# Attention: VectorE's lower parts from odd slots issued behind the next slot's softmax steps

## The chip, the cores and the metric

The kernel runs on one core of one Trainium2 chip. The metric is the device time of one execution in microseconds. Below, TensorE is also PE (matmuls) and PEld (its weight loads), VectorE is DVE, ScalarE is ACT, GpSimd is POOL, and SP is the engine that issues most DMAs. Each engine works through its own instructions in the order in which the program lists them.

## What is computed

Attention over 4 batches, 8 heads, 576 positions and head dimension 64, with a learned bias for each pair of positions, feeds a gated two-layer block over 2304 tokens:

```python
scores = scale * np.matmul(q, k.transpose(0, 1, 3, 2))
h = np.maximum(x @ w1 + b1, 0.0)          # x: log distance over log position
scores = scores + (h @ w2).transpose(2, 0, 1)[None]
attn = np.exp(scores - np.max(scores, axis=-1, keepdims=True))
attn = attn / (np.sum(attn, axis=-1, keepdims=True) + 1e-09)
out = np.matmul(attn, v)
...
gate = 1.0 / (1.0 + np.exp(-(x @ w_gate)))
return gate * (x @ w_val) @ w_out
```

## The kernel before

The program has three stages: the bias tables (to about 115 us), the attention (115 to about 405 us) and the gated block (from about 390 us to the end). The change touches the attention alone.

The attention works through 16 **units**, each a pair of heads of one batch, and each unit through 9 **slots** (`n = 9 * u + s`). The slots 0, 2, 4 and 6 compute the scores of two blocks of 128 rows, one for each head (12 matmuls of line 627 into two `sc` tiles); slot 8 computes the last 64 rows of both heads in one tile (6 matmuls of line 616); the odd slots compute no scores. There are two `sc` buffers, so the scores of a slot can start only when the softmax steps of the slot with scores before it have read theirs.

A **softmax step** (`soft`, lines 631 to 650) is, for one tile, a DVE instruction that adds the bias and takes the row's extreme (line 643, with a short read of the accumulator), for the second head a small addition (line 647), and the exponential with its row sum on ACT (line 648).

Two slots later `turn` brings the block's exponentials into the layout that the second product needs. Blocks of even slots and the one of slot 8 are transposed on PE (line 672, into one of three `pt` buffers); ACT writes the **upper part** in 16 bits to `at` (line 561), and DVE later writes the **lower part**, the rest (line 562). Blocks of odd slots (the second head's) are cut into two parts by POOL (lines 555 and 666, `cr`) and transposed by DMAs that SP issues (line 667). So of the lower parts that DVE writes, these come from odd slots: in slot 1 the two halves of the unit before's block 8; in slot 3 what `tail` issues for that unit (a lower part of 64 x 128 and the row sums' reciprocals `rt`, line 696, which SP stores to `rs`); in slots 5 and 7 the lower parts of V (`vv`, line 603), whose upper parts ACT writes on line 602 at the end of the slot.

The second product (line 732) of the unit before is spread over the slots in four groups of nine matmuls, 3 or 6 in a slot; each group fills the one `acc` buffer, which ACT empties to `xe` (line 736). The whole is written under a manual schedule: the order of the loop's code is the order on each engine.

Of the kernel before, what the change touches and what calls it, by code (L numbers as in the profile page):

```python
# [28 lines left out]
LAG, WSTEP, VSTEP, TAIL = 2, 2, (5, 7), 3  # L29
# [143 lines left out]
def tile_kernel(ctx, tc, q, k, v, small, w_gate, w_val, w_out, steps, lpos, xtab, lx, out, phases="0AB"):  # L173
# [7 lines left out]
    with ExitStack() as right, ExitStack() as att:  # L181
# [16 lines left out]

        sizes = {}
        attn = attention(tc, att, q, k, v, biases, biasL, ident, xs, rs, sizes, extra)  # L200
        next(attn)
        with tc.manual_schedule():
# [314 lines left out]
def attention(tc, att, q, k, v, biases, biasL, ident, xs, rs, sizes, extra):  # L517
# [15 lines left out]
    def load_k(u):  # L533

        p, b = units[u]
        qkraw[u, "kr"] = t = raw.tile([128, S], F32, name="kr")
        nc.sync.dma_start(out=t, in_=k[b, 2 * p:2 * p + 2].rearrange("h d s -> (h d) s"))

    def load_q(u):

        p, b = units[u]
        qkraw[u, "qr"] = t = raw.tile([128, S + 64], F32, name="qr")
        nc.sync.dma_start(out=t, in_=q[b, p].rearrange("h d s -> (h d) s"))

    def load_v(u):
        p, b = units[u]
        vraw[u] = raw.tile([128, 2, 5, D], F32, name="vr")
        nc.sync.dma_start(out=vraw[u], in_=v[b, p])
# [19 lines left out]
    def prep_k(u):  # L568
        kt[u] = t = two.tile([128, 2, S], F32R, name="k")
        pool_split(t[:, 0], t[:, 1], qkraw[u, "kr"])  # L570

    def prep_q(u):
        qt[u] = o = two.tile([128, 2, S + 64], F32R, name="part")
        pool_split(o[:, 0], o[:, 1], qkraw[u, "qr"])
# [23 lines left out]
    def split_v(u, h):  # L598
        if h == 0:
            vsplit[u] = vp.tile([128, 2, 5, 2, D], F16, name="vv")  # L600
        t, vv = vraw[u][:, h], vsplit[u][:, h]
        nc.scalar.activation(out=vv[:, :, 0], in_=t, func=AF.Copy, scale=sizes["up"])
        return lambda: nc.vector.scalar_tensor_tensor(out=vv[:, :, 1], in0=t, scalar=sizes["up"], in1=vv[:, :, 0], op0=ALU.mult, op1=ALU.subtract)
# [3 lines left out]
    def score(n):  # L607
        u, s = divmod(n, 9)
        ks, qs = kt[u], qt[u]
        if s == 0:  # L610
            state[u] = [st.tile([128, 9], F32, name="sm"), None, {}]
        if s == 8:
            ps = ps_s.tile([128, 2, 512], F32, name="sc")
            for i, (l, r) in enumerate(TERMS):
                for e in range(2):
                    nc.tensor.matmul(out=ps[:, e, 0:HF], lhsT=qs[:, l, 512:640], rhs=ks[:, r, HF * e:HF * e + HF],
                                     start=(i == 0), stop=(i == len(TERMS) - 1))
            return [soft(u, s, ps)]
        if s % 2:
            return []  # L620
        it = TURN[s][1]
        pair = [ps_s.tile([128, 2, 512], F32, name="sc") for _ in range(2)]
        for i, (l, r) in enumerate(TERMS):
            for e in range(2):
                for h in range(2):
                    rows = slice(64 * h, 64 * h + 64)
                    nc.tensor.matmul(out=pair[h][:, e, 0:HF], lhsT=qs[rows, l, 128 * it:128 * it + 128], rhs=ks[rows, r, HF * e:HF * e + HF],  # L627
                                     start=(i == 0), stop=(i == len(TERMS) - 1))
        return [soft(u, s + h, pair[h]) for h in range(2)]
# [22 lines left out]
    def turn(n):  # L652

        u, s = divmod(n, 9)
        p, b = units[u]
        if s == 0:
            state[u][1] = atp.tile([128, 2, 9, S], F16, name="at")
        sm, at, ens = state[u]
        h, it = TURN[s] if s < 8 else (0, 4)
        en = ens[4 * h + it if s < 8 else 8]  # L660
        i = slice(128 * it, 128 * it + 128)
        if s in CROSS:
            t = crp.tile([128, 2 * S], F16, name="cr")
            copy(t[:, 0:S], en)
            for a, z in ((640, slice(0, 512)), (S, slice(512, S))):
                nc.gpsimd.tensor_tensor(out=t[:, a:a + z.stop - z.start], in0=en[:, z], in1=t[:, z], op=ALU.subtract)  # L666
            crossed.append((n + LAG + XLAG, lambda: nc.sync.dma_start_transpose(out=at[:, h, :, i], in_=t)))
            return []
        after = []
        pt = ps_t.tile([128, 4, 128], F32, name="pt")  # L670
        for J in range(4):
            nc.tensor.transpose(pt[:, J], en[:, 128 * J:128 * J + 128], ident)  # L672
        if s == 8:
            return [split(at[:, h, 0:4, 512:576], at[:, h, 5:9, 512:576], pt[:, :, 64 * h:64 * h + 64]) for h in range(2)]
        after.append(split(at[:, h, 0:4, i], at[:, h, 5:9, i], pt))
        if it == 3:
            pt = ps_t.tile([128, 4, 128], F32, name="pt")
            for e in range(4):
                nc.tensor.transpose(pt[0:64, e], ens[4 * h + e][:, 512:576], ident)
            after.append(split(at[0:64, h, 4, 0:512], at[64:128, h, 4, 0:512], pt[0:64].rearrange("p e i -> p (e i)")))  # L680
        return after

    def tail(u):
        sm, at, ens = state[u]
        pt = ps_t.tile([128, 4, 128], F32, name="pt")
        nc.tensor.transpose(pt[0:64, 0], ens[8][:, 512:576], ident)
        last = normal(u, pt)
        return [split(at[0:64, :, 4, 512:576], at[64:128, :, 4, 512:576], pt[0:64, 0].rearrange("p (h i) -> p h i", h=2)), last]
# [14 lines left out]
    def invert(u):  # L703
        sm = state[u][0]

        def both():
            nc.vector.tensor_tensor(out=sm, in0=sm, in1=sizes["tiny"], op=ALU.add)
            nc.vector.reciprocal(out=sm, in_=sm)

        return both  # L710
# [35 lines left out]
    crossed = []  # L746
    with tc.manual_schedule():
        work = iter(())
        after, due, loads = [], [], []
        for n in range(9 * NU + LAG + 1):  # L750
            u, s = divmod(n, 9)
            softs = score(n) if n < 9 * NU else []
            inverse = invert(u - 1) if s == 0 and u > 0 else None
            later = turn(n - LAG) if LAG <= n < 9 * NU + LAG else []
            if s == TAIL and u > 0 or n == 9 * NU + LAG:
                later += tail(u - 1)
            if s == KSTEP and u + 1 < NU:
                prep_k(u + 1)
                if u + 2 < NU:
                    loads.append(lambda z=u + 2: load_k(z))  # L760
            if s == QSTEP and u + 1 < NU:
                prep_q(u + 1)
                if u + 2 < NU:
                    loads.append(lambda z=u + 2: load_q(z))
            for f in after:
                f()
            for f in due:
                f()
            for f in softs:
                f()  # L770
            due, loads = loads, []
            while crossed and (crossed[0][0] <= n or n == 9 * NU + LAG):
                crossed.pop(0)[1]()
            after = later
            if inverse:
                inverse()
            if s == WSTEP and 0 < u < NU:
                work = products(u - 1)
            if n == 9 * NU + LAG - 1:
                work = products(u - 1)  # L780
            for _ in range(FILL[s] if n < 9 * NU else 9 if n < 9 * NU + LAG else 0):
                f = next(work, None)
                if f:
                    f()
            if s in VSTEP and u < NU:
                after.append(split_v(u, VSTEP.index(s)))
                if s == VSTEP[1] and u + 1 < NU:
                    loads.append(lambda z=u + 1: load_v(z))
            extra(n)
        for f in after:  # L790
            f()
        for f in work:
            if f:
                f()
# [562 lines left out]
```

## Time and profile before

| | |
|---|---|
| time, median of 3 runs | 825.13 us (824.43 to 825.15) |
| the profiled execution's own time | 824.43 us, with a span of 822.6 us |
| PE, DVE, ACT, POOL busy over the span | 92%, 78%, 69%, 44% |
| attention's first and last softmax step on DVE | 114.7 us, 389.1 us |

The span is the part of the profiled execution in which engines work; what lies around it is 1.8 us. The busy shares are means over three stages with different limits, so the stage that is changed has to be read on its own. In the rows below that give busy time by stretch, the columns are the stretch, its length, the busy us (and instructions) of PE, PEld, DVE, ACT and POOL, then TensorE's granted clock, the DMA engines' busy share and GB/s.

### The profile page before, as it was taken

Reading aid. Unit: us, or ns where it says so; the run is one execution under the profiler, and the core shown is the slowest. Engines: PE = TensorE matmul, PEld = TensorE weight load, DVE = VectorE, ACT = ScalarE, POOL = GpSimd, SP = SyncE. Lnnn points to the kernel's source line nnn. Section 1 sums busy time; section 2 is a strip of 40 time slices with the busy share of each in tenths; the row PEclk is TensorE's granted clock in tenths of the full one; section 3 lists DMA queues with packets and bytes.
Section 4 is the critical chain, followed back from the end, with each engine's and each line's share of the span. In section 5 each row is a group of like instructions: output and inputs, shape, how many; then the busy total and the mean of one; then the engine's idle time right before and its main releaser. Section 6 shows DMA issues by size and latency. Waiting matters only on the chain. (4 is left out here: it accounts for less than half of the span.)

```text
span 822.6 us, 17293 instructions
## 1 busy us (share of the span) xinstructions
PE 756.1 (92%) x6343; PEld 548.1 (67%) x6343; DVE 642.6 (78%) x1362; ACT 564.6 (69%) x1206; POOL 362.8 (44%) x451
## 2 busy tenths in 40 slices
PE   7999878888888898788899999998999999999997
PEld 4888866666666666566799999984555555555553
DVE  6788877777778777888469889888998887777762
ACT  5887737877777777678657656476667666766553
POOL 2345448678777787784101111044743331533200
PEclk8999988999999999999999999999999999999999
DMA  5478315877687577886989884247621121522102
GB/s 193 152 192 186 108 44 140 161 161 169 145 180 165 142 178 168 212 210 157 245 295 285 248 227 133 90 138 210 180 93 64 60 77 47 184 78 78 52 1 77
DMA packets 137236, 121.84 MB, mean 148 GB/s; under 512 B 82368, under 2 KB 106048, under 8 KB 137152
## 3 DMA queue, kind: packets, MB, share of 16 engines
q1 hardware_dynamic: 130560, 112.03, 49.2%
q0 software_dynamic: 4672, 5.77, 4.8%
q10 hardware_dynamic: 1920, 2.95, 1.1%
q8 instruction: 49, 0.80, 0.4%
q14 instruction: 35, 0.29, 0.1%
HBM read 80.80 MB, written 23.67 MB: 127 GB/s over the span
## 5 line engine op out<-in xcount | busy, mean ns | idle before, releaser
L1158 PEld LDWEIGHTS <-wv 128*128 128x128 f16 x1008 | 98.1, 98 | 84.4 <-issue 9.4
L648 ACT ACTIVATE en<-en,mn 128x576 f32<-128x576 f32 x144 | 111.8, 777 | 57.6 <-DVE mn L643 55.8
L627 PE MATMUL sc<-k,part 64*128 64x288 f32 x768 | 95.8, 329 | 21.8 <-DVE mn L643 18.0
L1158 PE MATMUL pg<-xq,wv 128*128 128x384 f16 x576 | 109.3, 326 | 2.9 <-ACT c L1184 2.1
L1116 POOL TENSOR_TENSOR ws<-wm 128x256 f32<-128x256 f32 x44 | 43.5, 989 | 152.0 <-DMA wm<-scratch 151.3
L627 PEld LDWEIGHTS sc<-k,part 64*128 64x128 f32 x768 | 67.4, 195 | 50.6 <-DVE mn L643 43.5
L666 POOL TENSOR_TENSOR cr<-en,cr 128x512 f16<-128x512 f32 (+1 forms) x128 | 96.7, 776 | 5.3
L643 DVE CUSTOM_DVE_ANT_0 en<-sc,bias 128x576 f32<-128x576 f32 x128 | 91.3, 749 | 4.1 <-PE sc L627 3.7
L562 DVE SCALAR_TENSOR_TENSOR at<-pt,at 128x512 f16<-128x512 f32 (+3 forms) x128 | 71.3, 568 | 23.8 <-ACT at L561 19.9
L732 PE MATMUL acc<-at,vv 128*128 128x288 f16 x540 | 81.3, 287 | 7.2 <-ACT xe L736 6.2
L1005 PE MATMUL po<-wo,gh 128*128 128x512 f16 x288 | 85.7, 379 | 0.0
L1158 PE MATMUL pu<-xq,wv 128*128 128x384 f16 x432 | 82.0, 326 | 1.9 <-DVE c L1164 1.9
L1057 POOL DMA_DIRECT2D xt<-xs x32 | 27.2, 1093 | 110.7 <-DMA xt<-xs 110.5
L555 POOL TENSOR_SCALAR cr<-en 128x576 f16<-128x576 f32 x64 | 44.5, 695 | 67.9 <-DMA at<-cr 35.4
L732 PEld LDWEIGHTS <-vv 128*128 128x128 f16 x576 | 56.3, 98 | 26.3 <-issue 13.6
L1164 DVE TENSOR_TENSOR c<-pu,c 128x384 f32<-128x384 f32 x72 | 39.9, 554 | 42.3 <-PE pu L1158 29.1
L427 PE MATMUL bps<-cfs,ind 128*128 128x64 bf16 x1458 | 67.5, 193 | 3.2 <-DVE bias L443 1.7
L408 ACT ACTIVATE ind<-y 128x576 bf16<-128x576 f32 x100 | 62.4, 651 | 11.1 <-PE y L403 8.3
L427 PEld LDWEIGHTS <-ind 128*128 128x128 bf16 x1458 | 58.8, 98 | 9.7 <-issue 3.0
L561 ACT ACTIVATE at<-pt 128x512 f16<-128x512 f32 (+3 forms) x128 | 59.9, 493 | 5.1 <-PE pt L672 2.3
L1176 ACT ACTIVATE gh<-c 128x384 f16<-128x384 f32 x48 | 25.1, 523 | 53.9 <-DVE c L1174 52.5
L672 PE MATMUL pt<-ident,en 128*128 128x128 f32 x320 | 54.1, 293 | 1.4 <-ACT en L648 1.4
(179 smaller groups left out, 1746.2 us busy)
## 6 DMA issues: line engine op xcount, KB each, us to landing
wm<-scratch SPq DMA_DIRECT2D x48, 256.0 KB
xs<-xe SPq DMA_DIRECT2D x32, 288.0 KB
scratch<-wm SPq DMA_DIRECT2D x27, 256.0 KB
wo<-scratch SPq DMA_DIRECT2D x24, 256.0 KB
qr<-in_q_dram SPq DMA_DIRECT2D x16, 320.0 KB
vr<-in_v_dram SPq DMA_DIRECT2D x16, 320.0 KB
kr<-in_k_dram SPq DMA_DIRECT2D x16, 288.0 KB
xrec<-rs SPq DMA_DIRECT2D x48, 96.0 KB
```

The costliest lines, as they stand in the source:

```text
L408: nc.scalar.activation(out=o, in_=y[:, :, 0:HF], func=AF.Sigmoid, scale=float(2.0 ** 64))
L427: nc.tensor.matmul(out=o, lhsT=st, rhs=cfs[:, part], start=(part == 0), stop=(part == 2))
L561: nc.scalar.activation(out=hi, in_=ps, func=AF.Copy, scale=float(2.0 ** UP))
L562: return lambda: nc.vector.scalar_tensor_tensor(out=lo, in0=ps, scalar=float(2.0 ** UP), in1=hi, op0=ALU.mult, op1=ALU.subtract)
L627: nc.tensor.matmul(out=pair[h][:, e, 0:HF], lhsT=qs[rows, l, 128 * it:128 * it + 128], rhs=ks[rows, r, HF * e:HF * e + HF], start=(i == 0) ...
L643: nc.vector.tensor_tensor_reduce(out=half(en), in0=ps[:, :, 0:HF], in1=half(nbias), scale=-0.125, scalar=3.0e38, op0=ALU.add, op1=ALU.min, ...
L648: nc.scalar.activation(out=en, in_=en, func=AF.Exp, bias=mn, scale=-1.0, accum_out=sm)
L666: nc.gpsimd.tensor_tensor(out=t[:, a:a + z.stop - z.start], in0=en[:, z], in1=t[:, z], op=ALU.subtract)
L672: nc.tensor.transpose(pt[:, J], en[:, 128 * J:128 * J + 128], ident)
L732: nc.tensor.matmul(out=acc[:, 0:HF], lhsT=l, rhs=r, start=(i == 0), stop=(i == len(mms) - 1))
L1005: self.nc.tensor.matmul(out=po, lhsT=l[:, tt], rhs=r, start=(first and i == 0), stop=(last and i == 2))
L1158: nc.tensor.matmul(out=p, lhsT=W[i][:, l, at + kc], rhs=V[b][:, r, kc], start=(new and n == 0), stop=(n == 5), skip_group_check=not new)
```

## The change

In every slot the loop collects the functions that issue DVE's lower parts, and runs them in the next slot ahead of the softmax steps. After the change, those collected in odd slots are run in the next slot behind its softmax steps; those collected in even slots stay where they were.

```diff
-        after, due, loads = [], [], []
+        after, late, due, loads = [], [], [], []
...
             for f in due:
                 f()
-            for f in softs:
+            for f in softs + late:
                 f()
             due, loads = loads, []
             while crossed and (crossed[0][0] <= n or n == 9 * NU + LAG):
                 crossed.pop(0)[1]()
-            after = later
+            after, late = ([], later) if s % 2 else (later, [])
...
             if s in VSTEP and u < NU:
-                after.append(split_v(u, VSTEP.index(s)))
+                late.append(split_v(u, VSTEP.index(s)))
...
-        for f in after:
+        for f in after + late:
             f()
```

The instructions of ACT, POOL and SP stay in the order they had. On PE nothing moves inside the attention; one group of nine products of the last unit moves by three matmuls among the gated block's first ones. On DVE the rows below are of slots 5 to 8 of one unit before the change: `at<-pt` is a lower part, `vv` that of V, `en,mn<-sc` the softmax step's first instruction, with `biasL` that of slot 8.

```order
L562 SCALAR_TENSOR_TENSOR at<-pt,at 128x4x128
L603 SCALAR_TENSOR_TENSOR vv<-vr,vup,vv 128x5x64
L643 ISA en,mn<-sc,bias_72 128x576
L643 ISA mn 128x1
L643 ISA en,mn<-sc,bias_72 128x576
L643 ISA mn 128x1
L647 TENSOR_SCALAR mn<-mn 128x1
L562 SCALAR_TENSOR_TENSOR at<-pt,at 128x4x128
L603 SCALAR_TENSOR_TENSOR vv<-vr,vup,vv 128x5x64
L643 ISA en,mn<-sc,biasL 128x576
```

The same slots on DVE after the change:

```order
L562 SCALAR_TENSOR_TENSOR at<-pt,at 128x4x128
L643 ISA en,mn<-sc,bias_72 128x576
L643 ISA mn 128x1
L643 ISA en,mn<-sc,bias_72 128x576
L643 ISA mn 128x1
L647 TENSOR_SCALAR mn<-mn 128x1
L603 SCALAR_TENSOR_TENSOR vv<-vr,vup,vv 128x5x64
L562 SCALAR_TENSOR_TENSOR at<-pt,at 128x4x128
L643 ISA en,mn<-sc,biasL 128x576
L643 ISA mn 128x1
L603 SCALAR_TENSOR_TENSOR vv<-vr,vup,vv 128x5x64
```

Each `vv` now stands behind the softmax steps that it stood ahead of. On DVE, slots 2 to 4, before the change, from the second softmax step of slot 2 on; `64x2x64` and `rt` are what slot 3 issued:

```order
L643 ISA en,mn<-sc,bias_72 128x576
L643 ISA mn 128x1
L647 TENSOR_SCALAR mn<-mn 128x1
L562 SCALAR_TENSOR_TENSOR at<-pt,at 128x4x128
L562 SCALAR_TENSOR_TENSOR at<-pt,at 64x2x64
L696 TENSOR_SCALAR rt<-pt,vout 9x128
L643 ISA en,mn<-sc,bias_72 128x576
```

And after it, through the softmax steps of slot 4:

```order
L643 ISA en,mn<-sc,bias_72 128x576
L643 ISA mn 128x1
L647 TENSOR_SCALAR mn<-mn 128x1
L562 SCALAR_TENSOR_TENSOR at<-pt,at 128x4x64 x2
L562 SCALAR_TENSOR_TENSOR at<-pt,at 128x4x128
L643 ISA en,mn<-sc,bias_72 128x576
L643 ISA mn 128x1
L643 ISA en,mn<-sc,bias_72 128x576
L643 ISA mn 128x1
L647 TENSOR_SCALAR mn<-mn 128x1
L562 SCALAR_TENSOR_TENSOR at<-pt,at 64x2x64
L696 TENSOR_SCALAR rt<-pt,vout 9x128
```

The two halves of slot 1 have moved from ahead of slot 2's softmax steps to behind them, and the two instructions of slot 3 from ahead of slot 4's to behind them. On PE the matmuls at the border of slots 5 and 6 stand as they did; with what each waits for, after the change:

```order
L732 LDWEIGHTS vv
L732 MATMUL acc<-at,vv 128x288 [waits DVE_49]
L627 MATMUL sc<-k,part 128x288 [waits PE_49] x2
L627 MATMUL sc<-k,part 128x288 x10
L672 MATMUL pt<-ident,en 128x128 [waits Activation_49]
L672 MATMUL pt<-ident,en 128x128 x3
```

The first matmul here is the ninth of the second group, which needs the lower part of 64 x 128 (it waited for DVE before as well); the scores of slot 6 are behind it, and their own wait for DVE is covered by it now.

## Rows read from the trace of the kernel before

**Rows 1.** Who waited for whom, whole span: total us, times, longest us.

```profile
ACT en L648 <- DVE mn L643: 55.8, 74, 2.3
...
PEld sc L627 <- DVE mn L643: 43.5, 103, 1.8
...
DVE vv L603 <- ACT vv L602: 32.3, 31, 1.1
...
DVE en L643 <- PE sc L627: 3.7, 4, 1.6
```

**Rows 2.** DVE in order of time, one unit: start, duration, instruction, idle before.

```profile
181.78 0.76 DVE L643 CUSTOM_DVE_ANT_0 en<-sc,bias 128x576 f32<-128x576 f32 x1
...
184.89 0.76 DVE L562 SCALAR_TENSOR_TENSOR at<-pt,at 128x256 f16<-128x256 f32 x2 [0.71 <-ACT at L561]
185.56 0.75 DVE L643 CUSTOM_DVE_ANT_0 en<-sc,bias 128x576 f32<-128x576 f32 x1
...
188.34 0.28 DVE L562 SCALAR_TENSOR_TENSOR at<-pt,at 64x128 f16<-64x128 f32 x1 [0.41 <-ACT at L561]
...
188.93 0.73 DVE L643 CUSTOM_DVE_ANT_0 en<-sc,bias 128x576 f32<-128x576 f32 x1
...
192.22 0.77 DVE L603 SCALAR_TENSOR_TENSOR vv<-vr,vup,vv 128x320 f16<-128x320 f32 x1 [1.09 <-ACT vv L602]
192.91 0.74 DVE L643 CUSTOM_DVE_ANT_0 en<-sc,bias 128x576 f32<-128x576 f32 x1
...
...
196.21 0.55 DVE L603 SCALAR_TENSOR_TENSOR vv<-vr,vup,vv 128x320 f16<-128x320 f32 x1 [1.08 <-ACT vv L602]
196.68 0.75 DVE L643 CUSTOM_DVE_ANT_0 en<-sc,biasL 128x576 f32<-128x576 f32 x1
...
197.36 1.40 DVE L562 SCALAR_TENSOR_TENSOR at<-pt,at 128x512 f16<-128x512 f32 x2
198.79 0.76 DVE L643 CUSTOM_DVE_ANT_0 en<-sc,bias 128x576 f32<-128x576 f32 x1
```

**Rows 3.** ACT in order of time, slots 6 and 7 of that unit.

```profile
194.57 0.78 ACT L648 ACTIVATE en<-en,mn 128x576 f32<-128x576 f32 x1
...
195.34 0.39 ACT L736 ACTIVATE xe<-acc 128x288 f32<-128x288 f32 x1
195.63 0.55 ACT L602 ACTIVATE vv<-vr,vup 128x320 f16<-128x320 f32 x1
```

**Rows 4.** Busy time of each engine in stretches: the unit of rows 2, the 14th unit, attention's end.

```profile
181.78:198.79 17.01, 14.92 (x119) 10.90 (x117) 13.39 (x35) 13.13 (x32) 13.04 (x17) 1.00 0.76 159
...
332.71:353.22 20.51, 15.17 (x116) 10.91 (x116) 17.95 (x40) 13.55 (x34) 15.83 (x18) 1.00 0.89 212
...
388.43:410.00 21.57, 16.49 (x95) 14.39 (x94) 11.68 (x26) 13.28 (x32) 2.26 (x5) 0.92 0.99 242
```

**Rows 5.** PE and its weight loads in order of time, that unit.

```profile
183.28 0.81 PEld L627 LDWEIGHTS sc<-k,part 64*128 64x128 f32 x11 [0.31 <-DVE mn L643]
...
182.79 1.54 PE L627 MATMUL sc<-k,part 64*128 64x288 f32 x12
...
185.79 0.90 PE L732 MATMUL acc<-at,vv 128*128 128x288 f16 x6
186.62 1.49 PE L627 MATMUL sc<-k,part 64*128 64x288 f32 x12
```

**Rows 6.** DVE's softmax step of slot 8, in the first and the 13th unit.

```profile
128.85 0.74 DVE L643 CUSTOM_DVE_ANT_0 en<-sc,biasL 128x576 f32<-128x576 f32 x1
...
332.71 0.74 DVE L643 CUSTOM_DVE_ANT_0 en<-sc,biasL 128x576 f32<-128x576 f32 x1
```

**Rows 7.** Line 603: duration in ns, least, median, most, and first and last start.

```profile
L603 DVE SCALAR_TENSOR_TENSOR vv<-vr,vup,vv x32: 550/552/1324, 124.1 to 388.0; 128x320 f16<-128x320 f32 x32
```

**Rows 8.** POOL in order of time, that unit: its first wait and its last instructions.

```profile
181.10 0.67 POOL L555 TENSOR_SCALAR cr<-en 128x576 f16<-128x576 f32 x1 [3.83 <-DMA at<-cr]
...
192.74 1.53 POOL L666 TENSOR_TENSOR cr<-en,cr 128x512 f16<-128x512 f32 x2
```

## The prediction

> **What bounds the kernel now.** I read the waits first, then one unit of the attention on DVE, ACT and PE, then the busy time by stretch. In the sum of the waits [rows 1] ACT waits 55.8 us for the softmax step's first instruction on DVE, PE's weight loads 43.5 us for the same one, and DVE itself 32.3 us for ACT's upper part of V, 31 times, just over 1 us each. The other way round there is nearly nothing: the softmax step waits for PE's scores 3.7 us in all. So in the attention the scores lie ready, and DVE stands in front of them, held by something else in its queue.
>
> What holds it is seen in one unit [rows 2]. It takes 17.01 us, from slot 0's softmax step at 181.78 to the next unit's at 198.79. The steps of slots 2, 4, 6 and 8 start at 185.56, 188.93, 192.91 and 196.68, so the intervals are 3.78, 3.37, 3.98, 3.77 and 2.11 us. Ahead of four of the five stands an odd slot's instruction that waits for ACT: 0.71, 0.41, 1.09 and 1.08 us. From slot 6 to 8 the whole interval is one serial ring: softmax step on DVE, the second head's exponential on ACT from 194.57, `xe` at 195.34, `vv` at 195.63 to 196.18 [rows 3], DVE's `vv` at 196.21, and 0.47 us later the next softmax step. DVE has the scores all that time, and does nothing for 1.08 us of it.
>
> No engine is full in the unit: PE 14.92, DVE 13.39, ACT 13.13 and POOL 13.04 us of 17.01, at a granted clock of 1.00 [rows 4]. PE's figure is more than it needs, since matmuls that wait overlap with modelled ends.
>
> **The change, interval by interval.** Nothing is added or removed; what changes is what stands ahead of the softmax steps. I build the unit again with the durations of the rows, from slot 0's step as zero.
>
> *From slot 0 to slot 4, now 7.15 us.* Scores for slot 2 can start when both `sc` tiles are read; PE resumes at 183.28, 1.50 us after the first step's start, and the last of the twelve ends at 184.33 (182.79 + 1.54) [rows 5]. So slot 2's steps could start at 2.6 us instead of 3.78. Then PE becomes the limit: slot 4's scores stand behind the products of slots 2 and 3, which hang on ACT's release of `acc` and not on DVE; the six last begin at 185.79, and the scores behind them at 186.62, which is 4.84 after zero [rows 5]. That start stays. Twelve scores that need not wait take 0.05 us more than the eleven that start at 183.28 (1.05 us to the end at 184.33) and 0.1 for the first, so they are ready at about 6.0. On DVE, slot 2 has 1.5 us of steps, 0.1 of small addition, the two halves (0.67, from 184.89 to 185.56) and a whole lower part (0.70, half of 1.40): 2.6 + 3.0 = 5.6. PE ends last, 6.1 with the way to DVE. Gain 1.05.
>
> *From 4 to 6, now 3.98.* Behind 1.5 us of steps and 0.1 of addition now comes slot 3's lower part, 0.28 us. PE's ninth product of the second group waits for it, and slot 6's scores are queued behind that product, so this is a new wait: 1.9 us instead of 1.5, one product (0.12), twelve scores (1.15), 0.1 to reach DVE. That makes 3.3. Gain 0.7. SP's stores of `rt` come behind it too; behind them on SP stand the next load of q and a store of `xs`, both with a slot or more to spare.
>
> *From 6 to 8, now 3.77.* The ring is cut, since the `vv` of slot 5 has been ready on ACT long before slot 6's steps end. DVE's own queue is what is left: 1.6 + 0.47 + 0.70 = 2.75, while slot 8's six scores would be there earlier. With 0.25 for a meeting with POOL (below), 3.0. Gain 0.75.
>
> *From 8 to 0, now 2.11.* Here the change costs. Slot 8 has one step of 0.68 us, and behind it now stand slot 7's `vv` (0.47) and two lower parts (1.40) before the next unit's step: 2.6, 0.1 for gaps, and 0.25 again: 2.95. Loss 0.85.
>
> The sum is 1.05 + 0.7 + 0.75 - 0.85 = 1.65 us of a unit of 17.0.
>
> **The price I don't see.** The lower part of V takes 0.55 us at best, and 1.32 at most [rows 7]. POOL works without a pause from 181.10 to 194.27 [rows 8]; the `vv` of slot 7 at 196.21 falls into its pause now, and in a shorter unit it will not. So a meeting costs between nothing and 0.77 us for each of two `vv`. I take 0.25, nearer to the low end because the median is 0.55 although one `vv` of each unit falls into POOL's work already. At nothing the unit gains 2.15, at the full price 0.6.
>
> The Trainium skill has a rule for this in "SBUF — State Buffer", section "Who interferes with whom": a DVE instruction with two SBUF inputs contends with a GpSimd instruction that reads SBUF. By it both `vv` of a unit would meet POOL's instructions, and the sum would lie at the worse end, 0.6 a unit. The trace agrees only in part, since the median is the least duration.
>
> **The sum.** The slot 8 steps of the first and the 13th unit are at 128.85 and 332.71 [rows 6]: twelve intervals of 16.99 us. 12 x 1.65 = 19.8. The first unit gets half a unit's gain, 0.8. The last three units also carry the gated block's preparation: the 14th takes 20.51 us with DVE busy for 17.95 and the DMA engines for 0.89 of it [rows 4], so the waits there are partly filled with other work; I give each two thirds, 1.1, in all 3.3. The hand-over, where the DMA engines are busy for 0.99 of 388 to 410 us [rows 4], I price at nothing gained or lost; all behind it is the same work, started earlier. Total 23.9. The profiled execution took 822.6 in its span and 1.8 around it, 0.7 below the median of 825.13, so the same gain off the median gives 801.
>
> With the bounds of the `vv` price: 12 x 2.15 + 6 = 32, so 793; 12 x 0.6 + 2 = 9, so 816.
>
> **Rivals.**
> *Transposing DMAs become the bound.* POOL's first `cr` of a unit waits 3.83 us for a buffer that a transposing DMA releases, and then POOL works 13.17 us on end (181.10 to 194.27) [rows 8]. That is a slack of 3.8 in 17, and about 2 in 15.35. The DMA engines are busy 0.76 of the unit, 12.9 us [rows 4], which would be 0.84. If queueing makes the release come 1 us later for each unit than POOL could use it, beyond that slack, the unit is about 16.2: gain 0.8 on 15 units, 12 us, so 813. For it: shares of 0.89 went with the longest unit. Against: that unit also moved 212 GB/s instead of 159.
>
> *The units come down to an engine's floor.* With ACT at 13.13 and DVE at 13.39 us, a unit could shrink to 14 at most if the intervals overlapped better than my walk. 12 x 3 + 6 = 42: 783. Against it speak the single `acc` buffer and PE's queue, which my walk has.
>
> *ACT is the true bound and the waits only move.* Then DVE waits for ACT's upper parts of even slots instead, at the same rate, and the time stays at 825. ACT's order is untouched. Against it: ACT itself waits 55.8 us for DVE [rows 1].
>
> *Slower: the ninth product.* At slot 6 PE now waits for a lower part that DVE does behind two softmax steps, with the scores queued behind it. Price 0.5 us of each unit, 8 us in all, so 833. It decides if the waits that leave the front of the steps, 0.71, 0.41, 1.09 and 1.08 [rows 2], were hidden: if the steps could not start earlier than now. The 3.7 us of waiting for PE's scores [rows 1] speak against that.
>
> **Chances.** My walk, with `vv` between its bounds' middle parts (793 to 808): 0.63. Transposes or full meetings (809 to 818): 0.15. The floor (775 to 792): 0.09. The same: 0.06. Slower: 0.07. The range 788 to 816 holds the first, most of the second and part of the third, about 0.8. What a measurement can tell from no change is about 0.2%, 1.7 us; faster 0.87, within it 0.06, slower 0.07.
>
> **What the changed profile would show.** DVE's wait for ACT's `vv`, 32.3 us, all but gone, and ACT's wait for DVE's softmax step much lower than 55.8. The intervals of a unit near 2.6, 3.5, 3.3, 3.0 and 2.95, and 15.35 for the unit. In the interval of slot 8 to 0 the loss. `vv` with a mean between 0.6 and 0.9 us. New: PE waiting at slot 6 for DVE's lower part, and waits of the softmax step for PE's scores, above 3.7 us. POOL's wait for transposes down from 3.8 to about 2. The gated block from 430 us on as long as before. I am wrong if the unit stays above 16.2 (then POOL's wait for the transposes will have stayed or grown, or ACT will have no idle time), or if the hand-over takes several us more than the 21.57 us of before, because attention's transposes queue behind the weights' loads.

## The result, and the profile after

The changed kernel takes 802.32 us, median of four runs (800.0 to 804.4), where the kernel before took 824.78 beside it (822.19 to 825.15): a ratio of 0.9734 with an interval of 0.9695 to 0.9772, so 22.5 us or 2.7% faster. The profiled execution took 800.84 us, of which the span is 799.0.

The page's line of busy shares, of the changed kernel:

```profile
PE 735.8 (92%) x6343; PEld 539.5 (68%) x6343; DVE 650.3 (81%) x1362; ACT 555.4 (70%) x1206; POOL 360.1 (45%) x451
```

The counts and PE's share are those of before. Nothing was taken away, and no share says where 23 us went. The waits do; whole span of the changed kernel, total us, times, longest us:

```profile
POOL cr L555 <- DMA at<-cr: 32.8, 15, 4.7
...
ACT en L648 <- DVE mn L643: 22.6, 17, 2.2
ACT at L561 <- PE pt L672: 19.8, 32, 0.8
DVE en L643 <- PE sc L627: 19.1, 36, 1.1
...
PEld sc L627 <- DVE mn L643: 16.5, 34, 1.1
...
PEld sc L627 <- PE acc L732: 13.5, 14, 1.0
...
PE acc L732 <- DVE at L562: 10.7, 15, 2.7
```

Against [rows 1]: DVE's 32.3 us of waiting for ACT's upper part of V has no line any more, ACT's wait for the softmax step fell from 55.8 to 22.6 us, and that of PE's weight loads from 43.5 to 16.5. Two have come up. The softmax step now waits 19.1 us for scores (3.7 before), and PE waits 15 times, 10.7 us in all, for a lower part, with the scores queued behind that product; before, this wait has no line. The arrow has turned round: DVE, which stood in front of scores that lay ready, now often waits for them.

One unit of the changed kernel on DVE, start, duration, instruction, idle before, to be read beside [rows 2]:

```profile
173.64 0.76 DVE L643 CUSTOM_DVE_ANT_0 en<-sc,bias 128x576 f32<-128x576 f32 x1
...
176.21 0.76 DVE L643 CUSTOM_DVE_ANT_0 en<-sc,bias 128x576 f32<-128x576 f32 x1 [0.61 <-PE sc L627]
...
177.76 1.34 DVE L562 SCALAR_TENSOR_TENSOR at<-pt,at 128x256 f16<-128x256 f32 x3
179.68 0.76 DVE L643 CUSTOM_DVE_ANT_0 en<-sc,bias 128x576 f32<-128x576 f32 x1 [0.58 <-PE sc L627]
...
181.35 0.28 DVE L562 SCALAR_TENSOR_TENSOR at<-pt,at 64x128 f16<-64x128 f32 x1
...
182.99 0.76 DVE L643 CUSTOM_DVE_ANT_0 en<-sc,bias 128x576 f32<-128x576 f32 x1 [0.39 <-PE sc L627]
...
184.56 1.01 DVE L603 SCALAR_TENSOR_TENSOR vv<-vr,vup,vv 128x320 f16<-128x320 f32 x1
...
186.10 0.74 DVE L643 CUSTOM_DVE_ANT_0 en<-sc,biasL 128x576 f32<-128x576 f32 x1
...
186.77 1.20 DVE L603 SCALAR_TENSOR_TENSOR vv<-vr,vup,vv 128x320 f16<-128x320 f32 x1
187.89 1.39 DVE L562 SCALAR_TENSOR_TENSOR at<-pt,at 128x512 f16<-128x512 f32 x2
189.31 0.76 DVE L643 CUSTOM_DVE_ANT_0 en<-sc,bias 128x576 f32<-128x576 f32 x1
```

The five intervals are 2.57, 3.47, 3.31, 3.11 and 3.21 us, 15.67 in all instead of 17.01. No instruction that waited for ACT stands ahead of a step. Slot 8 to 0 is where the change costs: one step, then `vv` and two lower parts (186.77 to 189.28) before the next unit may begin. Both `vv` are stretched, to 1.01 and 1.20 us from the 0.55 that one takes at best.

PE of the changed kernel in that unit, at the border of slots 5 and 6:

```profile
179.96 1.14 PE L732 MATMUL acc<-at,vv 128*128 128x288 f16 x8
181.68 0.28 PE L732 MATMUL acc<-at,vv 128*128 128x288 f16 x1 [0.58 <-DVE at L562]
181.90 1.06 PE L627 MATMUL sc<-k,part 64*128 64x288 f32 x12
```

Eight products run, the ninth stands 0.58 us until DVE's 0.28 us piece at 181.35 is done, and only then come slot 6's scores. This is the new wait. PE of the kernel before at the same border ran all nine without one, and then began slot 6's scores:

```profile
188.66 1.26 PE L732 MATMUL acc<-at,vv 128*128 128x288 f16 x9
189.85 0.40 PE L627 MATMUL sc<-k,part 64*128 64x288 f32 x1
```

POOL of the changed kernel, its first `cr` of that unit and its last:

```profile
174.54 0.67 POOL L555 TENSOR_SCALAR cr<-en 128x576 f16<-128x576 f32 x1 [2.09 <-DMA at<-cr]
...
186.46 1.67 POOL L666 TENSOR_TENSOR cr<-en,cr 128x512 f16<-128x512 f32 x2
```

The wait for a transposing DMA is 2.09 us here (3.83 in [rows 8]); POOL ends at 188.13, 1.2 us before the next unit begins.

The same unit and the 14th, busy time by stretch, of the changed kernel:

```profile
173.64:189.31 15.67, 14.35 (x124) 11.16 (x123) 13.79 (x35) 12.44 (x32) 13.09 (x16) 1.00 0.88 170
308.98:327.90 18.92, 14.58 (x115) 10.89 (x114) 17.00 (x40) 14.14 (x36) 13.17 (x16) 0.91 0.95 231
```

DVE is now busy for 13.79 of 15.67 us, and the DMA engines' share went from 0.76 to 0.88.

Where the 23.6 us between the two spans lie, read from the starts of the slot 8 steps: the twelve intervals from 125.56 to 308.98 have a mean of 15.29 us instead of 16.99, 20.4 in all. The first unit, from its first step to its slot 8 step, takes 12.07 instead of 14.10, 2.0. The last three units take 53.46 instead of 55.72, 2.3. The attention's first step lies at 113.49 instead of 114.75: 1.3, which is not the change's, since nothing ahead of that step is changed (over the kernels below, it lies anywhere between 113.05 and 115.26). From the last slot 8 step to the end it takes 436.6 instead of 434.2 us: 2.4 lost. 20.4 + 2.0 + 2.3 + 1.3 - 2.4 = 23.6.

### The profile page after: what moved, and what is told of

Its sections match the earlier page's. It is cut to its first block, busy times and chain, and to the rows that moved or that the text cites. A ratio compares the mean times of both kernels' runs of the same rounds, so it can differ in the third digit from the quotient of the medians.

```text
span 799.0 us, 17293 instructions
## 1 busy us (share of the span) xinstructions
PE 735.8 (92%) x6343; PEld 539.5 (68%) x6343; DVE 650.3 (81%) x1362; ACT 555.4 (70%) x1206; POOL 360.1 (45%) x451
## 3 DMA queue, kind: packets, MB, share of 16 engines
q10 hardware_dynamic: 1920, 2.95, 1.1%
## 5 line engine op out<-in xcount | busy, mean ns | idle before, releaser
L1158 PEld LDWEIGHTS <-wv 128*128 128x128 f16 x1008 | 98.0, 98 | 85.5 <-issue 10.7
L648 ACT ACTIVATE en<-en,mn 128x576 f32<-128x576 f32 x144 | 110.8, 774 | 24.7 <-DVE mn L643 22.6
L643 DVE CUSTOM_DVE_ANT_0 en<-sc,bias 128x576 f32<-128x576 f32 x128 | 91.9, 755 | 21.5 <-PE sc L627 19.1
L732 PE MATMUL acc<-at,vv 128*128 128x288 f16 x540 | 84.1, 288 | 19.4 <-DVE at L562 10.7
L627 PEld LDWEIGHTS sc<-k,part 64*128 64x128 f32 x768 | 58.5, 189 | 43.1 <-DVE mn L643 16.5
L627 PE MATMUL sc<-k,part 64*128 64x288 f32 x768 | 78.3, 317 | 10.0 <-DVE mn L643 8.1
L562 DVE SCALAR_TENSOR_TENSOR at<-pt,at 128x512 f16<-128x512 f32 (+3 forms) x128 | 69.5, 564 | 5.8 <-ACT at L561 4.8
L561 ACT ACTIVATE at<-pt 128x512 f16<-128x512 f32 (+3 forms) x128 | 60.1, 496 | 19.9 <-PE pt L672 19.8
L555 POOL TENSOR_SCALAR cr<-en 128x576 f16<-128x576 f32 x64 | 45.3, 708 | 43.9 <-DMA at<-cr 32.8
```

What stands on the lines that cost most here:

```text
L561: nc.scalar.activation(out=hi, in_=ps, func=AF.Copy, scale=float(2.0 ** UP))
L562: return lambda: nc.vector.scalar_tensor_tensor(out=lo, in0=ps, scalar=float(2.0 ** UP), in1=hi, op0=ALU.mult, op1=ALU.subtract)
L643: nc.vector.tensor_tensor_reduce(out=half(en), in0=ps[:, :, 0:HF], in1=half(nbias), scale=-0.125, scalar=3.0e38, op0=ALU.add, op1=ALU.min, ...
L648: nc.scalar.activation(out=en, in_=en, func=AF.Exp, bias=mn, scale=-1.0, accum_out=sm)
L732: nc.tensor.matmul(out=acc[:, 0:HF], lhsT=l, rhs=r, start=(i == 0), stop=(i == len(mms) - 1))
L1158: nc.tensor.matmul(out=p, lhsT=W[i][:, l, at + kc], rhs=V[b][:, r, kc], start=(new and n == 0), stop=(n == 5), skip_group_check=not new)
```

## The experiments

The theory was that of the prediction: waits for ACT at the front of DVE's queue held scores that were ready; with them behind the steps, a unit falls to what DVE's and PE's own queues need. The rivals were the transposing DMAs as the bound, and a gain that comes from one of the moved pieces alone. Each time is a median of four executions (ten for the kernel before with four buffers). The kernel before took 825.33 us beside the first four kernels, 825.19 beside the next four and 824.47 beside the last four, and ratios are to these. Waits and intervals come from one traced execution each.

Intervals below are those of slots 0 to 2, 2 to 4, 4 to 6, 6 to 8 and 8 to 0, means over the second to the twelfth unit. Before the change they are 3.79, 3.37, 3.78, 3.85 and 2.11 us, with it 2.61, 3.41, 3.31, 2.97 and 3.01. The figure for a unit is the mean of the twelve intervals between slot 8 steps, 16.99 before and 15.29 with the change.

### Only V's lower parts behind the steps

```diff
-            after, late = ([], later) if s % 2 else (later, [])
+            after, late = later, []
```

> Only V's lower parts (slots 5 and 7) go behind the softmax steps; what slots 1 and 3 issue stays ahead. My walk: slot 0 to 4 stays at 7.15 us, 4 to 6 falls to about 2.7, 6 to 8 is 3.1, 8 to 0 rises to 3.15, so the unit is 16.1 and the time about 811. Rival 'all of the gain is the removed wait for ACT's V part' (32 us of waits): the whole gain of the change, about 802. Rival 'only the wait of slots 1 and 3 matters': about 825.

The kernel takes 805.92 us against 825.33, a ratio of 0.9766 (0.9737 to 0.9795), between the walk's 811 and the rival's 802. The intervals are 3.79, 3.49, 2.46, 2.92 and 2.91 us and a unit takes 15.56, so each of the last three intervals is some 0.2 shorter than expected. Waits of this kernel:

```profile
ACT en L648 <- DVE mn L643: 36.2, 43, 2.1
...
DVE at L562 <- ACT at L561: 26.0, 29, 5.1
...
DVE vv L603 <- ACT vv L602: 1.2, 6, 0.2
```

The wait of V is gone by this part alone. The other one at the front of DVE's queue, for ACT's `at`, is still there, and the first interval is as long as before. The interval of 4 to 6 fell by 1.3 us, to less than the whole change gives it, because here slot 3's piece stays ahead of the steps and PE's ninth product never waits for it.

### Only the pieces of slots 1 and 3 behind the steps

```diff
-                late.append(split_v(u, VSTEP.index(s)))
+                after.append(split_v(u, VSTEP.index(s)))
```

> Only what slots 1 and 3 issue goes behind the softmax steps; V's lower parts stay ahead. My walk: slot 0 to 4 falls to 6.1, 4 to 6 and 6 to 8 stay rings through ACT at about 3.85 and 3.77, 8 to 0 stays at 2.1, so the unit is 15.8 to 15.9 and the time about 809. Rival 'all is V': about 825, with the waits for V's part at 32 us as before.

The kernel takes 813.65 us, a ratio of 0.9862 (0.9831 to 0.9893), where the walk gave 809. The intervals are 2.61, 3.45, 4.20, 3.77 and 2.11 us, and a unit takes 16.15. Waits of this kernel:

```profile
DVE vv L603 <- ACT vv L602: 23.1, 30, 1.1
...
PE acc L732 <- DVE at L562: 10.7, 15, 2.0
```

Only the first interval gains. That of 4 to 6 becomes longer than before, 4.20 us where the walk had 3.85: PE's new wait is there in full, 10.7 us, and V's wait still follows it. The two parts alone gain 19.4 and 11.7 us, 31 together, and 22.5 as one. Most of the difference lies at 4 to 6: alone the parts change that interval by 1.32 - 0.42 = 0.90 us, and together they take 0.47 off it. The next kernel looks there.

### Slot 3's piece ahead of the steps again

```diff
-            after, late = ([], later) if s % 2 else (later, [])
+            after, late = ([], later) if s in (1, 5, 7) else (later, [])
```

> As the changed kernel, but slot 3's lower part and reciprocals go ahead of slot 4's steps again. My walk: in the changed kernel slot 6's scores wait behind a product that waits for this lower part; with it ahead, slot 4 to 6 falls from 3.3 to about 2.75 and slot 2 to 4 grows by at most 0.15, so the unit is 14.85 and the time about 795. Rival 'the product's wait is hidden': 802, no change against the changed kernel. Rival 'the wait for ACT ahead of slot 4 comes back in full': 0.4 us a unit, about 808.

The kernel takes 803.19 us, a ratio of 0.9739 (0.9699 to 0.9778): no better than the change, where the walk gave 795. The step did what was expected of it: 4 to 6 fell from 3.31 to 2.47, and PE's wait for DVE's `at` from 10.7 to 1.6 us. But the units came out uneven, 14.0 to 17.7 us with a mean of 15.09, and the last three took 55.74 together instead of 53.46. Waits of this kernel, and behind them a row of its PE:

```profile
POOL cr L555 <- DMA at<-cr: 28.5, 14, 4.5
...
PEld L732 <- DMA at<-cr: 13.9, 7, 3.4
...
PE acc L732 <- DMA at<-cr: 10.2, 5, 3.2
```

```profile
277.63 0.54 PE L732 MATMUL acc<-at,vv 128*128 128x288 f16 x3 [2.53 <-DMA at<-cr]
```

With the change PE's weight loads wait 4.4 us for transposing DMAs, three times; here 13.9 us, seven times. What one wait gave up, another took.

### Slot 7's V behind the next unit's first steps

Slot 7's `vv` is issued behind slot 0's steps, and the next load of V one slot later.

```diff
-        after, late, due, loads = [], [], [], []
+        after, late, last, due, loads = [], [], [], [], []
...
+            if s == 0:
+                while last:
+                    last.pop(0)()
...
-                late.append(split_v(u, VSTEP.index(s)))
-                if s == VSTEP[1] and u + 1 < NU:
-                    loads.append(lambda z=u + 1: load_v(z))
+                (late if s == VSTEP[0] else last).append(split_v(u, VSTEP.index(s)))
+            if s == 8 and u + 1 < NU:
+                loads.append(lambda z=u + 1: load_v(z))
```

> As the changed kernel, but the lower part of V that slot 7 issues goes behind the steps of the next unit's slot 0 (and the load of the next V one slot later). My walk: slot 8 to 0 falls from 3.1 to 2.2, slot 0 to 2 grows from 2.6 to about 2.8, unit 14.6 to 14.7, time about 793, and this instruction falls into POOL's pause, so its mean is under 0.7 us. Rival 'slot 8 to 0 is bound by PE, not by DVE's queue': no change, 802. Rival 'V's later load or the DMA transposes behind it become the bound': 805 or more, with POOL's wait for transposes above the 33 us of the changed kernel.

The kernel takes 802.15 us, a ratio of 0.9728 (0.9688 to 0.9768): again no better, where the walk gave 793. The moved `vv` came down to a mean of 0.60 us, as expected. But slot 8 to 0 fell only from 3.01 to 2.69 us, 0 to 2 rose from 2.61 to 2.83, and the last three units took 55.17 us together instead of 53.46. Weight loads wait 9.1 us for transposing DMAs, and POOL 33.4.

### Both of these edits, and three ways to relieve the transposes

> Both edits of the two runs before (slot 3's part ahead of slot 4's steps, slot 7's V part behind the next slot 0's steps). Theory 'transposing DMAs now bound the attention': 799 to 804, as each edit alone, with PE waiting for the transposes and some units of 16 us and more between units near 14. Theory 'DVE's order still bounds, and the two edits only disturbed each other's intervals': 788 to 794, units near 14.2 throughout.

With both edits the kernel takes 798.63 us, a ratio of 0.9673 (0.9635 to 0.9712), whose interval overlaps that of the change. The units lie between 13.35 and 17.83 us with a mean of 14.50, and the last three take 56.41 together. (The four executions spread from 794.33 to 800.75, and the traced one is the fastest.) POOL still waits 24.1 us for transposes and weight loads 11.0. So there is time to be had, and it is spread unevenly. What holds it was then taken apart on top of both edits. First a fourth buffer for the cut blocks:

```diff
-    crp = pool("crp", 3)
+    crp = pool("crp", 4)
```

> As the run with both edits, with four buffers for POOL's parts (cr) instead of three, so that POOL's first part of a unit no longer waits for the unit's first transpose. If the ring POOL, transposing DMA, POOL binds: POOL's wait for transposes falls from over 30 us to under 10 and the time to 788 to 795. If the DMA queue itself binds: POOL's wait falls, but PE's wait for the transposes stays or grows, and the time stays at 799 to 804.

The kernel takes 787.67 us, a ratio of 0.9548 (0.9528 to 0.9568). From the third interval between slot 8 steps to the twelfth every unit takes 14.13 to 14.34 us; the last three take 52.66 together. Waits of this kernel, and one of its units by busy time:

```profile
POOL cr L555 <- DMA at<-cr: 5.9, 3, 3.7
...
PEld L732 <- DMA at<-cr: 5.3, 2, 3.8
```

```profile
200.00:214.15 14.15, 13.61 (x117) 10.69 (x116) 13.47 (x36) 12.37 (x33) 12.85 (x17) 1.00 0.87 204
```

The transposes themselves are unchanged, and the DMA engines' share is 0.87 in a shorter unit, where the change had 0.88. So the bound was not the DMA engines' throughput, but the ring of POOL's cut, the transpose that reads it, and POOL's next cut into the same buffer. DVE with 13.47 of 14.15 us is next, and part of that is a meeting with POOL. DVE of this kernel in slots 6 to 8 of that unit:

```profile
207.73 0.76 DVE L643 CUSTOM_DVE_ANT_0 en<-sc,bias 128x576 f32<-128x576 f32 x1 [0.26 <-PE sc L627]
...
209.30 1.35 DVE L603 SCALAR_TENSOR_TENSOR vv<-vr,vup,vv 128x320 f16<-128x320 f32 x1
210.57 0.68 DVE L562 SCALAR_TENSOR_TENSOR at<-pt,at 128x512 f16<-128x512 f32 x1
211.17 0.74 DVE L643 CUSTOM_DVE_ANT_0 en<-sc,biasL 128x576 f32<-128x576 f32 x1
```

Slot 5's `vv` starts 0.17 us behind POOL's cut (209.13) and takes 1.35 us. From the second to the thirteenth unit it takes 1.33 to 1.35 each time but once, when it takes 1.52. DVE does not pause in this stretch, and the mean of 6 to 8 is 3.45 us, where the fourth buffer without the two edits has 2.73 (below). So the meeting with POOL is paid here, in the regular units too.

Then, with three buffers, the transposes' slot moved one earlier (`XLAG = 2` in place of 3):

> As the run with both edits, but each transposing DMA is issued one slot earlier on SP, so the unit's first goes ahead of a store of xs instead of behind it. If the place in SP's queue is what makes the transposes late: 788 to 796. If the DMA engines' own work binds: 799 to 804.

The kernel takes 793.92 us, a ratio of 0.9618 (0.959 to 0.9646). POOL's wait fell to 14.7 us and that of the weight loads to 2.1; the units keep a mean of 14.56, and the last three gain most, 51.03 together. It helps less than half as much as the buffer, and its interval overlaps that of both edits alone.

And with three buffers, q, k and V loaded for the first two units only; the loads of the others are left out, and the second unit's tensors stand in for them:

> As the run with both edits, but q, k and v are loaded for the first two units only and the second's are used for all that follow: about a third of the attention's DMA bytes are left out, and with them their place in the queue. If the DMA queue delays the transposes: units near 14.2 without the long ones, PE's wait for transposes gone, time 782 to 792. If POOL, ACT or PE bind at 15 us: 798 to 804.

The kernel takes 790.92 us, a ratio of 0.9591 (0.9569 to 0.9613). The weight loads no longer wait for a transpose, SP's issue of one takes a median of 1.35 us instead of 1.52, and the last three units take 51.13 us together instead of 56.41. But the other units stay at a mean of 14.54, and POOL still waits 23.2 us, 8.1 of them once at the attention's end. Between 227 and 287 us it waits 1.25 to 1.29 in every unit, and these units take 14.84 to 14.87. So other loads make transposes late, yet without them the ring still holds the units.

### The fourth buffer without the edits, and on the kernel before

> The changed kernel with four cr buffers and no other edit. If the ring POOL, transposing DMA, POOL only stretches some units of the changed kernel: units near 14.95 throughout instead of a mean of 15.29, POOL's wait for transposes near 6 us instead of 33, time 795 to 800. If the changed kernel's mean unit is DVE's order alone: no difference, 802.

The changed kernel with four buffers takes 797.15 us, a ratio of 0.9666 (0.9643 to 0.969). Nine of the twelve units take 14.73 to 14.82 us and three 15.12 to 15.37, with a mean of 14.87; the intervals are 2.58, 3.43, 3.31, 2.73 and 2.81. POOL waits no more for transposes. Against the change, only the two intervals with a `vv` have moved, by 0.24 and 0.20 us.

> The kernel before with four cr buffers. Its unit of 16.99 us should be set by DVE's waits for ACT, with POOL's wait for transposes hidden: 824 to 826, units as before. If the transposes' ring bound the kernel before as well: under 815.

The kernel before with four buffers takes 821.65 us, a ratio of 0.9967 (0.9951 to 0.9984). A unit takes 16.95 us, and DVE waits 32.4 us for ACT's upper part of V, as ever. These are some 3 us, where nothing was expected: before the change the ring was nearly free, and after it the same buffer gives 5.

> Both edits, four cr buffers, and each transpose one slot earlier on SP. Regular units stay at 14.15 (DVE, PE and ACT now set them), and the long 14th unit of 20 us falls towards 18, so 784 to 788. If the earlier issue makes SP wait for POOL: above 789.

Both edits, four buffers and transposes one slot earlier take 785.39 us (784.14 to 787.89), a ratio of 0.9527 (0.9499 to 0.9554). This is the lowest median, 17 us below the change; its interval overlaps that of both edits with the fourth buffer. From the third interval on units take 14.13 to 14.15 us, and what it has over that kernel lies in the last three, 50.66 instead of 52.66 together.

### V's lower part with one input

On the changed kernel with four buffers; the subtraction of the upper part is left out.

```diff
-        return lambda: nc.vector.scalar_tensor_tensor(out=vv[:, :, 1], in0=t, scalar=sizes["up"], in1=vv[:, :, 0], op0=ALU.mult, op1=ALU.subtract)
+        return lambda: nc.vector.tensor_scalar(out=vv[:, :, 1], in0=t, scalar1=sizes["up"], scalar2=None, op0=ALU.mult)
```

> The changed kernel with four cr buffers, but the lower part of V is computed as a scaled copy of V, without subtracting the upper part (that part of the computation is left out), so the instruction reads one tile of SBUF instead of two. If two SBUF inputs are what meets POOL: line 603 near its least duration in all 32 cases (median under 0.6 us), slot 6 to 8 at 2.7 and 8 to 0 at 2.65 us, units about 0.6 us shorter than in the run with four buffers alone, time 787 to 792. If any DVE instruction beside POOL is stretched: median 0.8 us and more, same time as the run with four buffers.

The kernel takes 792.78 us, a ratio of 0.9624 (0.9594 to 0.9654). Below is line 603's duration in ns, least, median and most, of the changed kernel, of it with four buffers, and of this one:

```profile
L603 DVE SCALAR_TENSOR_TENSOR vv<-vr,vup,vv x32: 537/902/1902, 124.1 to 363.1; 128x320 f16<-128x320 f32 x32
```

```profile
L603 DVE SCALAR_TENSOR_TENSOR vv<-vr,vup,vv x32: 550/590/1268, 125.9 to 359.6; 128x320 f16<-128x320 f32 x32
```

```profile
L603 DVE TENSOR_SCALAR vv<-vr,vup x32: 535/539/543, 123.3 to 355.0; 128x320 f16<-128x320 f32 x32
```

With one input the duration never varies, although it still falls into POOL's cuts. The units did not get shorter for it, 14.84 against 14.87: with four buffers most of the stretch had already left DVE, so the 0.6 us of a unit that were expected were not there to be had. The medians are 4.4 us apart, and the traced executions 7.8: 1.7 lie ahead of the attention, 1.3 in the first unit, 0.4 in the twelve, 1.2 in the last three, and 3.2 behind them. In the kernel with both edits and four buffers, where the meeting does stand in DVE's queue, one input was not tried.

## Why the prediction was right

The forecast of 801 us was off by 1.3, and the mechanism is shown, not only the size: the wait that the change removes is gone by V's part alone in one run and stands in full in the run without it, and each moved piece changed its own interval. By its steps, in us:

| step | forecast | measured |
|---|---|---|
| slot 0 to 4 | 6.1 | 6.02 (2.61 + 3.41) |
| 4 to 6 | 3.3 | 3.31 |
| 6 to 8 | 3.0 | 2.97 |
| 8 to 0 | 2.95 | 3.01 |
| unit | 15.35 | 15.29 |
| twelve units | 19.8 gained | 20.4 |
| first unit | 0.8 gained | 2.0 |
| last three units | 3.3 gained | 2.3 |
| hand-over and all behind | 0 | 2.4 lost |
| ahead of the attention | 0 | 1.3 gained, not by the change |

**The walk.** All four steps came within 0.1. In slot 0 to 4 PE ends last, as said: DVE's step waits 0.61 and 0.58 us for scores. In 4 to 6 the wait of the ninth product was priced at 0.4 us (1.9 instead of 1.5), and in the unit shown it comes out as 0.58 with the scores behind it. Undoing that piece alone gave its 0.84 us back.

**The price of a meeting.** I took 0.25 for each `vv`. Two readings bear on it. The instruction itself is longer by more, a median of 902 ns, 0.35 us above 0.55. The intervals with it fall by 0.24 and 0.20 when four buffers let POOL run freely and the median falls to 590 ns. So the term was right in the interval, but my reason for it was not. I read the median of 552 ns in [rows 7] as few meetings. The trace of before has a meeting in most units: in nine of the sixteen the `vv` of slot 5 starts 0.06 us ahead of POOL's cut (226.60 and 226.66 in one of them), and the cut is the one that takes longer, 1.77 us instead of 1.43. POOL paid, in its slack. After the change POOL is later against the softmax steps (in the two units shown, its cut behind the long wait starts 0.90 us behind slot 0's step instead of 0.68 ahead of it), and the cut is under way when `vv` comes. The worse end of the sum, a gain of 0.6 a unit, did not come. The Trainium skill, "SBUF — State Buffer", section "Who interferes with whom", states that a DVE instruction with two SBUF inputs contends with a GpSimd one that reads SBUF, and that one with at most one SBUF input, outside the two-port modes, does not. The last experiment agrees (535 to 543 ns with one input). The same section of the Trainium skill states that issue order decides who blocks; the trace of before agrees, with 1.77 us for POOL where `vv` started first.

**The mis-sized terms** lie at the edges: 1.2 us too little for the first unit, 1.0 too much for the last three, and 2.4 of loss where I had put nothing. Without the 1.3 us ahead of the attention, which nothing in the change explains, the spans would differ by 22.3 and not 23.6. That the sum of 23.9 comes so close to the latter is in part luck. The first unit had both waits of V before, 1.07 and 0.79 us, and I gave it half a unit's gain. The last three gave 0.8 each instead of 1.1. The hand-over lost: from the last slot 8 step to the first matmul of the gated block it takes 9.92 us instead of 8.51, and 1.0 more is lost behind that. Over the other kernels the first stretch takes 6.5 to 10.4 us, and the changed kernel with four buffers has 7.96 there but loses 3.4 more behind it, 438.0 in all against 436.6. No experiment took the two apart; the cause stays open.

**The rivals.** The transposing DMAs were not the outcome, but a part of it: they make the unit 15.29 on average and up to 16.29, where the four buffers have 14.75 nearly throughout, and they took nearly all that two further edits had to give. The floor of an engine (14 us) was nearly reached with both edits and the fourth buffer, at 14.15. ACT as the true bound fell: its wait for DVE dropped by 33 us, and no wait of DVE for ACT's even slots took its place (4.8 us in all). The ninth product costs 10.7 us of PE's waits, which the earlier steps pay several times over.

**What the profile was to show** came as listed but for the gated block, which is 1.0 us longer behind its first matmul: `vv` with a mean of 0.88 us lies in 0.6 to 0.9, and POOL's wait in the unit shown is 2.09 of "about 2". Over the whole span that wait only went from 35.4 to 32.8 us, though, 15 times instead of 12, which already told of the next bound.

## What to carry to other kernels

In an in-order queue, look at what stands in front of work that is ready: a wait of about 1 us by an off-path instruction cost more than the step itself (0.75 us), and no engine's busy share told of it. When the instruction is moved, ask who waits for its result and what is queued behind that waiter, and price it; here the new wait was 0.6 us of a unit, with 2.5 gained in three intervals and 0.9 lost in a fourth. When a cut wait gives less than its size, look for a ring through a buffer next: one more buffer was worth 3 us before the change, 5 after it and 11 after two more edits.

## What the runs showed of the hardware

**Who comes second pays the meeting.** DVE's and POOL's rows of the changed kernel with four buffers, one unit:

```profile
216.18 0.57 DVE L603 SCALAR_TENSOR_TENSOR vv<-vr,vup,vv 128x320 f16<-128x320 f32 x1
...
218.09 0.55 DVE L603 SCALAR_TENSOR_TENSOR vv<-vr,vup,vv 128x320 f16<-128x320 f32 x1
```

```profile
215.25 1.67 POOL L666 TENSOR_TENSOR cr<-en,cr 128x512 f16<-128x512 f32 x2
...
218.15 1.78 POOL L666 TENSOR_TENSOR cr<-en,cr 128x512 f16<-128x512 f32 x2
```

At 218.09 `vv` starts 0.06 us ahead: it takes 0.55, and POOL's pair 1.78 instead of 1.43. At 216.18 `vv` is 0.93 us behind the start of POOL's pair, whose first instruction takes 1.16; it takes 0.57, and here too the pair is longer, 1.67, in its second instruction, which comes behind `vv`. In the changed kernel's unit above `vv` starts 0.31 us behind POOL (186.77 after 186.46) and takes 1.20; in the kernel with both edits and four buffers it starts 0.17 behind and takes 1.35. With one input, POOL of that kernel:

```profile
214.82 1.43 POOL L666 TENSOR_TENSOR cr<-en,cr 128x512 f16<-128x512 f32 x2
```

DVE's `vv` started 0.27 us ahead of it there (214.55, 0.54 us) and neither is longer. A shift of some tenths of a microsecond between two engines thus moves the price from one to the other.

**A wait of PE was followed by the lower clock.** In the 14th unit of the changed kernel PE's weight loads wait for a transposing DMA, and the matmul itself for ACT's upper part; the two waits end within 0.05 us of each other. PEld, PE, and the stretches around it (with the granted clock behind POOL's column):

```profile
324.43 1.81 PEld L732 LDWEIGHTS <-vv 128*128 128x128 f16 x9 [3.28 <-DMA at<-cr]
```

```profile
324.44 2.34 PE L732 MATMUL acc<-at,vv 128*128 128x288 f16 x9 [3.04 <-ACT at L561]
```

```profile
322.00:324.00 2.00, 0.00 (x0) 0.00 (x0) 2.00 (x5) 0.79 (x3) 2.00 (x2) 0.97 1.20 239
324.00:326.00 2.00, 1.56 (x7) 1.01 (x8) 1.97 (x5) 1.94 (x5) 1.92 (x3) 0.50 0.90 281
326.00:328.00 2.00, 2.00 (x13) 1.81 (x11) 0.60 (x2) 0.86 (x2) 1.92 (x4) 0.67 0.96 208
```

PE did nothing from 321.4 to 324.44 us. ACT's upper part was late in its turn: the instruction ahead of it on ACT had waited 1.21 us for a load of V. So an earlier transpose alone would not have ended this pause sooner. The granted clock is then 0.50, the lower level of 1.2 GHz, and nine products take 2.34 us, where eight and one took 1.14 and 0.28 in the unit above. So this wait cost PE its 3 us and about one more.
